# The last Fourier step of a spectral layer: each product in two halves of 64 columns, on two column tiles

## The chip, the cores and the metric

The kernel runs on one core of a Trainium2 chip. Its time is the device time of one execution in microseconds (us). The time before is a median of three runs; the profile is of one further execution. TensorE (PE) multiplies matrices: a weight load (LDWEIGHTS, shown as PEld) puts the stationary operand into the array, and a matmul then streams the moving operand through it into a PSUM bank. VectorE (DVE), ScalarE (ACT) and GpSimd (POOL) do the elementwise work, and SyncE (SP) starts the transfers (DMA).

## The reference

The input x has 8 batches of 3008 positions with 256 channels. Two layers follow each other: a mixing of the channels in the frequency domain, and a gated feed-forward network on each of the 24064 positions.

```python
X = np.fft.rfft(x, axis=1)
Yr = Xr @ w_r - Xi @ w_i + b_r
Yi = Xr @ w_i + Xi @ w_r + b_i
Yr = np.sign(Yr) * np.maximum(np.abs(Yr) - lam, 0.0)
Yi = np.sign(Yi) * np.maximum(np.abs(Yi) - lam, 0.0)
y = np.fft.irfft(Yr + 1j * Yi, n=3008, axis=1)
g = y @ w_gate
out = (g / (1 + np.exp(-g)) * (y @ w_val)) @ w_out
```

## The kernel before

The Fourier transforms are products with constant matrices. A length of 3008 is 47 times 64, so each transform has two steps. Forward: `stage_a` (line 395) transforms over 47 values with the weights `wa`; a transpose on DVE (line 400) turns the result; `second` (line 432) transforms over 64 values with `wf`. In the frequency domain two lines mix the channels (`total_product`, line 439, and `mix`, line 454), ACT gathers (line 466), and DVE and POOL clip and shrink (lines 499 and 500). Backward: `back` (lines 476 and 478) goes back over 64 values, the result is stored to a DRAM tensor `d2` in the order of frequencies k1, and `product` in `unit` (line 541) goes back over the 24 values of k1. This last one is the inverse over k1.

One unit of the inverse over k1 handles one batch b and one group u of four values of m (UM = 4, NU = 8 groups). It loads `z_in` from `d2`: 96 partitions (24 values of k1, real and imaginary parts, two halves) by 4 x 256 columns (four m, 256 channels). For each half cc of the channels, `product(cc)` then makes four matmuls, one for each m: the stationary operand is z_in with 128 channels as its columns, the moving operand are 94 columns of the constant `wo` for this m, and the result is 128 channels (partitions) by 94 positions, in a bank of its own (`ps_x0` or `ps_x1`), where the four matmuls lie beside each other. `copy(cc)` (line 552) copies the 376 columns of the bank to SBUF on ACT, and one transfer for both halves (line 565) writes them to `xt_d`, from where the feed-forward part reads its input. All operands of line 541 are f32, and in the program one f32 product of this kind is two weight loads and two matmuls. Batches 0 to 6 pass through `unit`: 7 x 8 units, 112 calls of `product`, 448 products. The last batch goes another way, in `inverse` (line 890) within the feed-forward part; there the same kind of product stays as it is.

The order of the first part is written out by a planner (`Plan`): each step has an engine, a cost, a due time and the steps that it needs. The steps of the inverse over k1 are "third0 n" and "third1 n" on PE, with a planned cost of 0.9, "xt0 n" and "xt1 n" on ACT, and "z_in n" and "out n" on SP. "third" needs the loaded z_in and the copy of the unit before out of the same bank; "xt" needs "third". The planner lays the steps out by these costs, and the kernel issues them in that order under a manual schedule. From the step "second 95" on (LOOSE = 95), the steps are issued outside the manual schedule. The feed-forward part (`gated_ffn`, products in line 655) begins where the transforms end; it reads what `xt_d` holds.

Of the kernel before, what the change touches and what calls it, by code (L numbers as in the profile page):

```python
# [17 lines left out]
P = 128  # L18
B = 8
SEQ = 3008  # L20
C = 256
# [225 lines left out]
def transform(ctx, tc, front, ring, last, ps_, feed, xp, w_r, w_i, cb, wup_raw, wdn_raw, ca, cf, ci, co, w21, wup_d, wdn_d, xt_d, d2):  # L247
    nc = tc.nc
# [276 lines left out]
    def unit(n):  # L525

        b, u = divmod(n, NU)
        key = (Z_FIRST + n * NP / NU if n < Z_LATE else Z_AT + (n - Z_LATE) * Z_STEP) * SLOT
        made = {}
        rows = d2.get(b)  # L530

        def load():
            t = made["z_in"] = last.tile([P, UM * C], F32, name="z_in", tag="z_in", bufs=3)
            rows = d2[b].rearrange("k (q m) c -> (k q) (m c)", m=NM)
            nc.sync.dma_start(t[:96], rows[:, u * UM * C : (u + 1) * UM * C])

        def product(cc):
            ps = made[cc] = ps_.tile([P, T], F32, name=f"ps_x{cc}")
            for i in range(UM):
                m = u * UM + i  # L540
                nc.tensor.matmul(  # L541
                    ps[:, i * 94 : (i + 1) * 94],
                    lhsT=made["z_in"][:96, i * C + cc * P : i * C + (cc + 1) * P],
                    rhs=box["wo"][:, m * 94 : (m + 1) * 94],
                    start=True,
                    stop=True,
                )

        def copy(cc):
            if "xt" not in made:  # L550
                made["xt"] = last.tile([P, 2, UT], F32, name="xt", tag="xt")
            nc.scalar.copy(made["xt"][:, cc, :], made[cc][:, :UT])

        old = lambda name, i: f"{name} {n - i}" if n >= i else None
        plan.add(f"z_in {n}", "SP", 0.5, key - 1.5 * SLOT, [f"store {b * NP + NP - 1}", old("third1", 3), "wo" if not n else None], load, 5.5)
        for cc in range(2):
            plan.add(f"third{cc} {n}", "PE", 0.9, key + (0.6 + 0.15 * cc) * SLOT, [f"z_in {n}", old(f"xt{cc}", 1)] + ([f"third0 {n}"] if cc else []), lambda cc=cc: product(cc))
            plan.add(f"xt{cc} {n}", "ACT", 0.36, key + (0.8 + 0.15 * cc) * SLOT, [f"third{cc} {n}", old("out", 2)] + ([f"xt0 {n}"] if cc else []), lambda cc=cc: copy(cc))
        plan.add(
            f"out {n}",  # L560
            "SP",
            0.45,
            key + 1.2 * SLOT,
            [f"xt1 {n}"],
            lambda: nc.sync.dma_start(xt_d[b][:, :, u * UT : (u + 1) * UT], made["xt"]),
            4.0,
        )

    box = {}
# [412 lines left out]
```

## Time and profile before

| What | Value |
|---|---|
| median of 3 runs | 2637.27 us (2637.2 to 2637.51) |
| the profiled execution: time | 2638.41 us |
| the profiled execution: span of its instructions | 2636.6 us |
| mean granted TensorE clock | 0.999 |
| line 541 in the stretch from 117 to 590 us: matmul records | 896, 115.25 us busy |
| line 541 in the same stretch: weight loads | 896, 111.44 us busy |
| line 655 (feed-forward), largest group of matmuls | 4032, 1038.1 us busy |
| line 890 (last batch), matmul records | 128, 18.1 us busy |

Times in the profile count from the start of the span. Matmul and weight-load records overlap each other, since the array is pipelined; the busy time of a group is the sum of the lengths of its records and may be longer than the time in which they pass. How far two starts lie apart tells what one of them really holds. A form such as "96*128 96x94" reads: 96 rows and 128 columns of the array in use, and 96 partitions by 94 elements streamed.

### The profile page before, as it was taken

What the parts mean: (1) busy time and instruction counts of PE and PEld (TensorE: products, weight loads), DVE (VectorE), ACT (ScalarE), POOL (GpSimd) and SP (SyncE); (2) the same over time, 40 slices, a digit from 0 to 9 for tenths busy, and PEclk for the clock granted to TensorE, in tenths of its full rate; (3) what the DMA queues carried; (4) which work ended last, traced back from release to release, by engine and by line L of the source; (5) the groups of instructions that cost most, each with busy time, mean ns of one, the idle gap of its engine ahead of it and who ended that gap; (6) DMA issues with size and microseconds to landing.
All of it is one profiled execution on the core that took longest, in us unless ns stands there. A gap on an engine that the chain in (4) does not pass through costs nothing.

```text
span 2636.6 us, 39325 instructions
## 1 busy us (share of the span) xinstructions
PE 2624.9 (100%) x13170; PEld 2206.3 (84%) x13170; DVE 2087.7 (79%) x3033; ACT 1713.4 (65%) x3344; POOL 2048.2 (78%) x1574
## 2 busy tenths in 40 slices
PE   9999999999999999999999999999999999999999
PEld 6888888898888888888888888888888888888899
DVE  6998788657787778777877878787878887888787
ACT  4777777786666666666666666656666666666665
POOL 3666665457888888888888888888888888888886
PEclk9999999999999999999999999999999999999999
DMA  6577766765544454445444444454444444444453
GB/s 191 180 257 231 235 226 224 242 196 195 182 165 151 149 165 158 153 145 165 164 149 149 164 166 154 145 165 165 146 145 161 160 152 150 151 159 159 150 176 127
DMA packets 141402, 452.54 MB, mean 172 GB/s; under 512 B 13776, under 2 KB 61616, under 8 KB 141104
## 3 DMA queue, kind: packets, MB, share of 16 engines
q1 hardware_dynamic: 141200, 450.02, 51.2%
q8 instruction: 105, 1.72, 0.3%
q14 instruction: 97, 0.79, 0.1%
HBM read 359.01 MB, written 90.96 MB: 171 GB/s over the span
## 4 chain that ended last, share of the span: by engine, by line
PE 98%; ACT 1%; DVE 0%; DMA 0%; POOL 0%; issue 0%; SPq 0%; ACTq 0%; DVEq 0%
PE bank L655 76%; PE mixb L454 5%; PE ps_a L395 4%; PE ps_x L541 4%; PE ps_b L432 3%; PE ps_s L439 3%; PE ps_z L478 2%; PE bank L890 1%; ACT hidden L800 0%; DMA x_first<-xp 0%; PE ps_z L476 0%; ACT t L466 0%; DVE f_lo L492 0%; DVE y_lo L502 0%; DVE wsum L299 0%
## 5 line engine op out<-in xcount | busy, mean ns | idle before, releaser
L655 PE MATMUL bank<-x_near,wup 128*128 128x512 f32 (+1 forms) x4032 | 1038.1, 386 | 0.6 <-DVE bank L829 0.3
L675 POOL TENSOR_TENSOR h_parts<-more,h_parts 128x512 fp32r<-128x512 f32 (+1 forms) x572 | 847.6, 1494 | 110.5 <-ACT h_parts L671 96.9
L655 PEld LDWEIGHTS bank<-x_near,wup 128*128 128x128 f32 x4032 | 750.5, 188 | 152.2 <-DVE bank L829 4.2
L655 PE MATMUL bank<-h_parts,wdn 128*128 128x512 f32 (+1 forms) x3021 | 835.7, 385 | 0.4 <-DVE h_parts L675 0.4
L675 POOL TENSOR_TENSOR h_parts<-hidden,h_parts 128x512 fp32r<-128x512 f32 (+1 forms) x431 | 564.9, 1322 | 206.4 <-ACT h_parts L671 187.0
L655 PEld LDWEIGHTS bank<-h_parts,wdn 128*128 128x128 f32 x3021 | 564.6, 188 | 109.3 <-DVE h_parts L675 0.7
L671 ACT CAST h_parts<-hidden 128x512 fp32r<-128x512 f32 (+1 forms) x433 | 266.0, 615 | 450.3 <-DVE hidden L802 450.3
L655 PE MATMUL bank<-x_parts,wup 128*128 128x512 f32 (+1 forms) x2016 | 526.6, 384 | 0.0
L802 DVE TENSOR_TENSOR hidden<-hidden,bank 128x512 f32<-128x512 f32 (+1 forms) x576 | 376.2, 675 | 77.8 <-PE bank L655 69.5
L655 PEld LDWEIGHTS bank<-x_parts,wup 128*128 128x128 f32 x2016 | 375.1, 188 | 71.5 <-DVE bank L829 1.8
L696 DVE TENSOR_TENSOR sums<-sums,bank 128x512 f32<-128x512 f32 (+1 forms) x357 | 240.4, 673 | 243.2 <-PE bank L655 243.2
L671 ACT CAST h_parts<-more 128x512 fp32r<-128x512 f32 (+1 forms) x572 | 349.6, 611 | 39.4 <-DVE more L666 28.1
L800 ACT ACTIVATE hidden<-bank 128x512 f32<-128x512 f32 (+1 forms) x432 | 252.7, 585 | 114.2 <-PE bank L655 113.9
L666 DVE TENSOR_TENSOR more<-hidden 128x512 f32<-128x512 f32 (+1 forms) x286 | 292.1, 1060 | 0.0
L666 DVE TENSOR_TENSOR more<-hidden,more 128x512 f32<-128x512 f32 (+1 forms) x286 | 258.3, 903 | 0.0
L500 POOL TENSOR_TENSOR t<-t,y 128x512 f32<-128x512 f32 x96 | 129.8, 1352 | 139.5 <-DVE y L499 132.9
L807 ACT COPY bank<-bank 128x512 f32<-128x512 f32 (+1 forms) x288 | 161.6, 561 | 109.2 <-DVE hidden L802 103.8
L829 DVE TENSOR_TENSOR bank<-hidden,bank 128x512 f32<-128x512 f32 (+1 forms) x288 | 197.0, 684 | 37.9 <-PE bank L655 26.0
L466 ACT COPY t<-mixb 64x256 f32<-64x256 f32 x384 | 141.2, 368 | 58.8 <-PE mixb L454 53.9
L815 ACT COPY hidden<-bank 128x512 f32<-128x512 f32 (+1 forms) x288 | 167.6, 582 | 2.5
L494 POOL TENSOR_TENSOR f_lo<-f,f_hi 128x256 fp32r<-128x256 f32 x96 | 90.8, 946 | 79.9 <-ACT f_hi L493 78.0
L214 POOL TENSOR_TENSOR x_near<-xf,x_near 128x512 fp32r<-128x512 f32 (+1 forms) x112 | 143.1, 1293 | 5.6 <-PE bank L655 4.8
(102 smaller groups left out, 3339.6 us busy)
## 6 DMA issues: line engine op xcount, KB each, us to landing
wup<-wup_d SPq DMA_DIRECT2D x288, 896.0 KB, 4.6
out<-o SPq DMA_DIRECT2D x88, 256.0 KB, 6.0
scratch<-xp SPq DMA_DIRECT2D x116, 192.0 KB, 3.2
d<-z SPq DMA_DIRECT2D x84, 256.0 KB, 2.6
z_in<-d SPq DMA_DIRECT2D x56, 384.0 KB, 3.7
xt_d<-xt SPq DMA_DIRECT2D x56, 376.0 KB, 3.9
xf<-xt_d SPq DMA_DIRECT2D x15, 1024.0 KB, 6.7
wup_d<-wup SPq DMA_DIRECT2D x12, 896.0 KB, 4.4
```

The lines of the kernel that those rows point to most:

```text
L214: low = lambda: eng.tensor_tensor(part[:, 1, :h], src, f32(part[:, 0, :h]), op=ALU.subtract)
L466: nc.scalar.copy(t()[64 * half : 64 * half + 64, k * C : (k + 1) * C], mixb[64 * k : 64 * k + 64, half * C : (half + 1) * C])
L655: nc.tensor.matmul(o, lhsT=weights[w], rhs=parts[x], start=start and i == 0, stop=stop and i == 2, skip_group_check=True)
L666: v.tensor_tensor(at(o, h), at(a, h), at(b, h), op=ALU.subtract)
L671: act.copy(pair[i][:, 0, :h], at(i, h))
L675: eng.tensor_tensor(pair[i][:, 1, :h], at(i, h), f32(pair[i][:, 0, :h]), op=ALU.subtract)
L696: v.tensor_tensor(o, o, spare[:, :h], op=ALU.add)
L800: act.activation(at(i, h), src, AF.Silu)
L802: v.tensor_tensor(at(i, h), at(i, h), src, op=ALU.mult)
L807: act.copy(b3[:, :h], b1[:, :h])
L815: act.copy(m5, b2[:, :h])
L829: v.tensor_tensor(b2[:, :h], m5, b3[:, :h], op=ALU.add)
```

## The change

Each product of line 541 is made as two, of 64 columns of z each. The first writes partitions 0 to 63 of the bank, the second partitions 64 to 127; the start of the output's partitions sets the column tile of the array on which a matmul runs. Both stream the same 94 columns of `wo`. The operands, the result, the copy out of the bank and the planned costs stay as they are. The order is: both records of the first half, then both of the second, then the next m.

```diff
             for i in range(UM):
                 m = u * UM + i
-                nc.tensor.matmul(
-                    ps[:, i * 94 : (i + 1) * 94],
-                    lhsT=made["z_in"][:96, i * C + cc * P : i * C + (cc + 1) * P],
-                    rhs=box["wo"][:, m * 94 : (m + 1) * 94],
-                    start=True,
-                    stop=True,
-                )
+                for side in range(2):
+                    col = i * C + cc * P + 64 * side
+                    nc.tensor.matmul(
+                        ps[64 * side : 64 * side + 64, i * 94 : (i + 1) * 94],
+                        lhsT=made["z_in"][:96, col : col + 64],
+                        rhs=box["wo"][:, m * 94 : (m + 1) * 94],
+                        start=True,
+                        stop=True,
+                    )
```

## The prediction

> **What bounds the kernel now.** I read the page first, for the share of each engine and for the chain of work that ended last.
>
> ```profile
> span 2636.6 us, 39325 instructions
> PE 2624.9 (100%) x13170; PEld 2206.3 (84%) x13170; DVE 2087.7 (79%) x3033; ACT 1713.4 (65%) x3344; POOL 2048.2 (78%) x1574
> PE 98%; ACT 1%; DVE 0%; DMA 0%; POOL 0%; issue 0%; SPq 0%; ACTq 0%; DVEq 0%
> PE bank L655 76%; PE mixb L454 5%; PE ps_a L395 4%; PE ps_x L541 4%; PE ps_b L432 3%; PE ps_s L439 3%; PE ps_z L478 2%; PE bank L890 1%; ACT hidden L800 0%; DMA x_first<-xp 0%; PE ps_z L476 0%; ACT t L466 0%; DVE f_lo L492 0%; DVE y_lo L502 0%; DVE wsum L299 0%
> ```
>
> TensorE carries 98% of the chain, and line 541, the only line that the change touches, has 4% of it: about 105 us. The first question is then where line 541 runs, and whether anything but TensorE holds that stretch. The view of one line gives its first and last start, the view of windows the busy time there, and the view of the tile ps_x the copies that read its results.
>
> ```profile
> L541 PEld LDWEIGHTS ps_x<-wo,z_in x896: 187/192/192, 117.6 to 588.6; 96*128 96x128 f32 x180
> L541 PE MATMUL ps_x<-wo,z_in x896: 244/275/275, 117.8 to 588.7; 96*128 96x94 f32 x180
> ```
>
> ```profile
> 117.00:590.00 473.00, 472.89 (x3361) 420.42 (x3360) 364.79 (x608) 362.16 (x842) 279.27 (x261) 1.00 0.70 228
> ```
>
> ```profile
> L552 ACT COPY xt<-ps_x x112: 464/473/507, 119.0 to 590.2; 128x376 f32<-128x376 f32 x112
> ```
>
> The columns of the window row are length, then PE, PEld, DVE, ACT and POOL busy, granted clock, DMA share and GB/s. From 117 to 590 us TensorE is busy for 472.89 of 473.00 us at a granted clock of 1.00; DVE (364.79) and ACT (362.16) have over 100 us to spare. So time added on TensorE here is added to the end in full, and time saved there is saved up to what the other engines allow. The 112 copies of line 552 are 112 blocks of line 541 (seven batches, eight groups, two channel halves); each block makes 4 products, and 896 matmul records are 8 a block. One f32 product is therefore two pairs of a weight load and a matmul.
>
> Now the inside of a block. The timeline of the matmuls (start, length, group, count), then the weight loads of the same block:
>
> ```profile
> 200.65 0.28 PE L454 MATMUL mixb<-wm_lo,f_hi 128*128 128x256 f32 x1
> 200.77 1.03 PE L541 MATMUL ps_x<-wo,z_in 96*128 96x94 f32 x8
> 201.58 0.48 PE L478 MATMUL ps_z<-y_hi,wi_hi 128*128 128x512 f32 x1
> ...
> 202.35 1.03 PE L541 MATMUL ps_x<-wo,z_in 96*128 96x94 f32 x8
> 203.22 1.13 PE L432 MATMUL ps_b<-wf,d 128*128 128x128 f32 x8
> ```
>
> ```profile
> 200.65 0.98 PEld L541 LDWEIGHTS ps_x<-wo,z_in 96*128 96x128 f32 x8
> ```
>
> ```profile
> 200.77 0.36 PE L541 MATMUL ps_x<-wo,z_in 96*128 96x94 f32 x2
> ```
>
> A record is 0.275 us long but they overlap, so what counts is the distance of the starts. From the first matmul of a block to the first of the next line: 201.58 - 200.77 = 0.81 us, and 203.22 - 202.35 = 0.87 us in the other; 112 blocks of these are 91 to 97 us. The weight loads follow each other every (0.98 - 0.19) / 7 = 0.113 us. The last row is a shorter window onto the same block, showing its first two matmuls: the second starts 0.36 - 0.275 = 0.085 us after the first. Its weights were loaded ahead, behind the previous line's matmul. So streaming 94 f32 columns holds the array for 0.085 us, loading 128 f32 columns of weights takes 0.113 us, and **line 541 is bound by its weight loads**, not by its streams. Each pair wastes about 0.028 us of the stream.
>
> **The change part by part.** Each product becomes two, of 64 columns of z each, into partitions 0 to 63 and 64 to 127 of the same bank. Per block, 8 pairs become 16: 896 weight loads and 896 matmuls more over the kernel. The 94 columns of wo are streamed once for each half. DMAs, copies, waits and the order of the blocks written out by the plan stay as they are, and the data read and written are the same; the copy of line 552 still waits for the block's last matmul. No wait and no queue entry on another engine is added. Everything therefore hangs on three unknown prices on TensorE. Every matmul of this trace is 128 columns wide, so none of the three is shown.
>
> First, the **weight load of 64 columns**. Below stands half of the present one, 0.113 / 2 = 0.0565 us, above the same 0.113 us (if the price did not hang on the columns). The nearest row for the dependence is the same for 96 and 128 rows, with equal columns:
>
> ```profile
> L541 PEld LDWEIGHTS ps_x<-wo,z_in 96*128 96x128 f32 x896 | 111.4, 191 | 2.2
> L432 PEld LDWEIGHTS ps_b<-wf,d 128*128 128x128 f32 x768 | 102.7, 196 | 16.6 <-issue 9.7 <-ACT f_hi L493 2.2 <-DVE d L400 0.5
> ```
>
> Rows change the mean by 5 ns only (191 against 196), so the columns are what is left to carry it, and I take half. Two halves loaded in turn then cost what one whole costs now: 4 x 0.0565 = 0.226 us a product against 2 x 0.113 = 0.226 us, a change of 0. The Trainium skill, page "TensorE: Matmul & The Clock Gate", section "LDWEIGHTS (loading the stationary operand)", also has the time go by columns and not by rows; by its rate, 128 columns are 0.107 us (measured here: 0.113 us) and 64 would be an estimated 0.053 us. That is the Trainium skill's figure, and the sum by it is the same to 1 or 2 us.
>
> Second, the **streams**. If the two halves can be streamed side by side, in program order, a product's four matmuls (high and low part of half 0, then of half 1) take two stream times, since the low part of one half and the high part of the next fall together: 2 x 0.085 = 0.17 us, and the loads at 0.226 us still bind unless they too run side by side. If the halves take turns, it is 4 x 0.085 = 0.34 us. The ends are thus -0.056 us a product (448 x 0.056 = -25 us) and +0.114 us (448 x 0.114 = +51 us; counted by blocks, 15 x 0.085 + 0.06 = 1.335 against 0.81 us, 112 x 0.525 = +59 us, which I use). I take the middle case, streams that overlap and loads in turn: 0, since the streams (0.17 us) lie behind the loads (0.226 us); without that cover it is the second end. A gain beyond -25 us is excluded by the order of the matmuls.
>
> Third, the **passage from full width to half width and back**, at both ends of each block. Going from line 454 (128 rows) to line 541 (96 rows) costs nothing now: 200.77 - 200.65 = 0.12 us, which is the spacing inside line 454 as well. Leaving costs 0.06 us: the last matmul starts at 200.77 + 1.03 - 0.275 = 201.525, the next line at 201.58. So one end is 0. The other end is a wait until the array has emptied: the next matmul starts only when the record before it ends.
>
> ```profile
> L454 PE MATMUL mixb<-wm_lo,f_hi 128*128 128x256 f32 x384 | 108.4, 282 | 0.0
> L541 PE MATMUL ps_x<-wo,z_in 96*128 96x94 f32 x896 | 115.2, 271 | 0.0
> ```
>
> Entering: 0.282 - 0.12 = 0.16 us. Leaving: 0.275 - 0.06 = 0.215 us. Together 0.38 us a block, 112 x 0.38 = **+42 us**; were the next weight load to wait as well (some 0.1 us at either end), up to 112 x 0.6 = +67 us. The row change is the nearest passage in the trace and is free, but in it the 128 columns remain one array. Here the columns are divided, weights still waiting for full width and weights for half width would lie in the array together, and the ends of the overlapping records are as far as their work reaches. I take +42 us. The Trainium skill, page "TensorEngine Tiling (Array Packing)", section "Key Properties", states that changing the tiling mode, as against the tile, drains TensorE. No run here shows it yet. It speaks against this change.
>
> The sum: loads 0, streams 0, passages +42 us. The profiled execution took 2638.41 us (its span is 2636.6 us), 1.1 us over the median of 2637.27 us; the sum is 2638.4 + 42 = 2680.4 us there, and 2637.3 + 42 = 2679 us as a median. I say 2680 us. The last blocks, some 18 after 550 us, lie partly where the scheduler and not the written order places them, and could stand differently; at 0.4 us each that is worth a few us.
>
> **The rivals.** (1) **Side by side, and no price for the passage**: loads of the two halves run beside each other too, the product takes 0.17 us, 448 x -0.056 = -25 us, 2612 us. This one ends on the other side: faster. It decides wherever the passages cost less than 25 / 112 = 0.22 us a block. DVE and ACT leave room for it (364.79 and 362.16 us of 473). For it speaks the measured 0.028 us of each pair in which the stream waits for weights; against it, that no row shows two loads under way closer than 0.11 us. The Trainium skill, page "TensorE: Matmul & The Clock Gate", section "Part 3: Packing small matmuls — row/col tiling", has matmuls on different column tiles run at once; by the Trainium skill it would thus be this case or the forecast, and not the third. No run here shows it. (2) **Streams overlap, loads in turn, free passage**: 0, 2637 us. With side-by-side loads but the passage at +42 us: -25 + 42 = +17 us, 2654 us. (3) **The halves take turns**, so the change does not do what the two column tiles say: +59 us, 2696 us. For it speaks that in the whole of the quoted block no two matmuls start closer than 0.085 us. (4) Turns and passages: +59 + 42 = +101 us, 2738 us; the same +101 us comes if a load keeps its 0.113 us whatever its width (8 x 0.113 = 0.90 us a block more).
>
> **How the numbers follow.** The forecast (2680 us, its own range 2650 to 2705 us by the passage at 0.1 to 0.6 us) has 0.32. Rival 1 (2612) has 0.23; a free passage with loads in turn (2637) 0.11; loads beside each other with the passage paid (2654) 0.09; turns (2696) 0.16; turns and passages, or loads of unchanged price (2738), 0.09. What can be told from no change is about 0.2%, 5 us. Faster: rival 1 and a little of the mixed cases, 0.24. Same: the free passage, 0.12. Slower: the rest, 0.64. The range goes from 2610 us to 2720 us, so that it leaves out the last case alone.
>
> **What would show it.** In the changed kernel line 541 should have 1792 weight loads and 1792 matmuls of 64 columns. In the timeline of one block: a forecast that holds shows starts about 0.056 us apart on average inside the block, and 0.28 us or so between the last matmul before the block and its first, likewise behind it. Rival 1 shows an inside of 0.65 us for 16 matmuls and 0.06 to 0.12 us at the ends; turns show 0.085 us throughout. TensorE must stay at its 473 of 473 us with a longer stage, and the stage after 590 us must keep its length of 2046 us. The prediction is wrong if the ends of the blocks show no gap, or if the stage's length does not follow from the blocks, above all if the sequencer cannot deliver twice as many instructions and gaps of "issue" appear in front of them; the present trace cannot say, since 0.113 us a pair is its densest stretch.

## The result, and the profile after

The change makes the kernel slower: 2651.21 us (median of 4 runs, 2650.91 to 2652.39) against 2637.39 us, a ratio of 1.0053 with a 95% interval of 1.0036 to 1.0070, or +13.8 us. The profiled execution took 2650.91 us, with a span of 2649.1 us, 12.5 us more than before. The sign was forecast, the size was not: +42 us stood in the prediction.

The page of the changed kernel; line 543 is now what line 541 was, and line 657 what line 655 was.

```profile
span 2649.1 us, 41116 instructions
PE 2637.6 (100%) x14066; PEld 2186.9 (83%) x14066; DVE 2085.2 (79%) x3033; ACT 1712.5 (65%) x3344; POOL 2046.4 (77%) x1574
PE 98%; ACT 1%; DVE 0%; DMA 0%; issue 0%; SPq 0%; ACTq 0%; DVEq 0%
PE bank L657 76%; PE mixb L454 5%; PE ps_a L395 4%; PE ps_b L432 4%; PE ps_x L543 3%; PE ps_s L439 3%; PE ps_z L478 3%; PE bank L892 1%; ACT hidden L802 0%; DMA x_first<-xp 0%; PE ps_z L476 0%; DVE f_lo L492 0%; ACT t L466 0%; DVE d L400 0%; DVE bank L853 0%
```

TensorE bounds the kernel as before, and 896 matmuls and as many loads were added. What stands out is that line 543 has *less* of the chain (3%) than line 541 had (4%), although the kernel is slower. The view of windows (length, then busy time of PE, PEld, DVE, ACT and POOL) shows where the time lies: the stage with line 543 now ends at about 602 us, 12 us later, TensorE is busy in it all the time, and what follows is as long as it was.

```profile
117.00:602.00 485.00, 484.60 (x4251) 399.70 (x4249) 363.65 (x607) 362.88 (x840) 277.81 (x261) 1.00 0.69 222
602.00:2646.00 2044.00, 2041.75 (x9208) 1703.13 (x9204) 1628.78 (x2277) 1277.88 (x2336) 1711.99 (x1257) 1.00 0.47 158
```

One block in the timeline of the matmuls (start, length, group, count), to be set beside the block shown in the prediction:

```profile
258.25 0.28 PE L454 MATMUL mixb<-wm_lo,f_hi 128*128 128x256 f32 x1
258.45 0.87 PE L543 MATMUL ps_x<-wo,z_in 96*64 96x94 f32 x16
259.26 0.86 PE L432 MATMUL ps_b<-wf,d 128*128 128x128 f32 x5
```

Inside, 16 matmuls take 0.87 us where 8 whole ones took 1.03 us: the block itself is shorter. At its ends it loses. From the last matmul before the block to its first are 258.45 - 258.25 = 0.20 us (0.12 us before the change). From the block's last start, 258.45 + 0.87 - 0.244 = 259.08, to the next line are 0.18 us. Before the change that depended on the line behind: 0.06 us with line 478, as in the block of the prediction, and 0.11 us with line 432. So a block with lines 454 and 478 around it is the one to compare:

```profile
333.91 0.28 PE L454 MATMUL mixb<-wm_lo,f_hi 128*128 128x256 f32 x1
334.12 0.87 PE L543 MATMUL ps_x<-wo,z_in 96*64 96x94 f32 x16
334.92 0.50 PE L478 MATMUL ps_z<-y_hi,wi_hi 128*128 128x512 f32 x1
```

The whole visit, from the last start before it to the first start behind it, takes 334.92 - 333.91 = 1.01 us against 201.58 - 200.65 = 0.93 us: 112 x 0.08 = +9 us. The next start behind is late as well: where line 432 follows it comes 0.22 us after the first in place of 0.15 us, elsewhere 0.02 us later than before. Counted up to this second start, and over all whole blocks of the two traces, a visit has grown from 1.19 to 1.29 us: 112 x 0.10 = +11 us.

Shorter windows onto the block at 258.45 us, two of the matmuls and two of the weight loads, show how it becomes shorter:

```profile
258.45 0.30 PE L543 MATMUL ps_x<-wo,z_in 96*64 96x94 f32 x2
...
258.45 0.38 PE L543 MATMUL ps_x<-wo,z_in 96*64 96x94 f32 x4
```

```profile
258.45 0.14 PEld L543 LDWEIGHTS ps_x<-wo,z_in 96*64 96x64 f32 x2
...
258.45 0.20 PEld L543 LDWEIGHTS ps_x<-wo,z_in 96*64 96x64 f32 x4
```

Two matmuls, the longest of them 0.295 us, end 0.30 us after the first start: in the nanoseconds of the trace they start 7 ns apart. So do their two loads, which are 0.133 us long and over in 0.14 us. **Streams and loads of the two column tiles run side by side.** Four loads are over in 0.20 us, the last of them 0.136 us long, so that the second pair of loads starts 0.06 us behind the first: a load of 64 columns holds its tile for about half of the 0.113 us of a whole one. The next pair of matmuls follows 0.13 us after the first, all further pairs about every 0.080 us, so that a product, two pairs, takes 0.16 us where it took 0.223 us.

A count over the whole trace: the distance from each matmul's start to the next one's, summed by the lines at which it begins and ends (us; "the line" is line 541 or its successor).

| Kernel | within the line | into it | out of it | other transform lines | feed-forward |
|---|---|---|---|---|---|
| before | 83.9 | 16.5 | 8.1 | 476.8 | 2045.2 |
| after | 70.6 | 28.5 | 20.3 | 479.5 | 2044.0 |
| after less before | -13.3 | +11.9 | +12.2 | +2.7 | -1.1 |

The last row adds up to 12.5 us before rounding, the whole growth of the span. Most of the +2.7 us is the passage once more, the late second start behind a block: 24 x 0.07 = 1.7 us where line 432 follows. After 570 us, where the order is not the written one, other lines break into some blocks: the traces have 114 visits before the change and 118 after it.

### The profile page after: what moved, and what is told of

Same layout as the page of the kernel before. It is cut to its first block, busy times and chain, and to the rows that moved or that the text cites. A ratio compares the mean times of both kernels' runs of the same rounds, so it can differ in the third digit from the quotient of the medians.

```text
span 2649.1 us, 41116 instructions
## 1 busy us (share of the span) xinstructions
PE 2637.6 (100%) x14066; PEld 2186.9 (83%) x14066; DVE 2085.2 (79%) x3033; ACT 1712.5 (65%) x3344; POOL 2046.4 (77%) x1574
## 4 chain that ended last, share of the span: by engine, by line
PE 98%; ACT 1%; DVE 0%; DMA 0%; issue 0%; SPq 0%; ACTq 0%; DVEq 0%
PE bank L657 76%; PE mixb L454 5%; PE ps_a L395 4%; PE ps_b L432 4%; PE ps_x L543 3%; PE ps_s L439 3%; PE ps_z L478 3%; PE bank L892 1%; ACT hidden L802 0%; DMA x_first<-xp 0%; PE ps_z L476 0%; DVE f_lo L492 0%; ACT t L466 0%; DVE d L400 0%; DVE bank L853 0%
```

## The experiments

Eight kernels were run, each beside the kernel before; their ratios are to that.

| Run | median us | ratio, 95% interval |
|---|---|---|
| after | 2651.2 | 1.0053, 1.0036 to 1.0070 |
| both channel halves in one step, halves of z | 2632.5 | 0.9983, 0.9974 to 0.9992 |
| both channel halves in one step, whole products | 2637.2 | 1.0000, 0.9991 to 1.0008 |
| both in one step, first channel half alone in halves of z | 2642.7 | 1.0019, 1.0010 to 1.0028 |
| every other product in halves | 2698.0 | 1.0228, 1.0214 to 1.0242 |
| quarters | 2648.2 | 1.0042, 1.0029 to 1.0055 |
| both in one step, quarters | 2631.4 | 0.9976, 0.9967 to 0.9985 |
| loops exchanged | 2693.2 | 1.0212, 1.0198 to 1.0225 |
| two products a side | 2656.7 | 1.0071, 1.0059 to 1.0084 |

**Fewer passages, the same work.** Theory A is that each passage to and from half width costs, and the block itself gains; theory B that the doubled number of instructions costs. A unit's two channel halves are made in one step, so that 32 half-width matmuls stand together and there are 56 visits in place of 112.

```diff
-        for cc in range(2):
-            plan.add(f"third{cc} {n}", "PE", 0.9, key + (0.6 + 0.15 * cc) * SLOT, [f"z_in {n}", old(f"xt{cc}", 1)] + ([f"third0 {n}"] if cc else []), lambda cc=cc: product(cc))
-            plan.add(f"xt{cc} {n}", "ACT", 0.36, key + (0.8 + 0.15 * cc) * SLOT, [f"third{cc} {n}", old("out", 2)] + ([f"xt0 {n}"] if cc else []), lambda cc=cc: copy(cc))
+        plan.add(f"third1 {n}", "PE", 1.8, key + 0.6 * SLOT, [f"z_in {n}", old("xt1", 1)], lambda: [product(cc) for cc in range(2)])
+        for cc in range(2):
+            plan.add(f"xt{cc} {n}", "ACT", 0.36, key + (0.8 + 0.15 * cc) * SLOT, [f"third1 {n}", old("out", 2)] + ([f"xt0 {n}"] if cc else []), lambda cc=cc: copy(cc))
```

> The changed kernel with both channel halves of a unit made in one step, so that 56 blocks of 32 half-width matmuls stand in place of 112 blocks of 16; instructions and operands are the same. Theory A (the passage between full and half width costs 0.09 us at the entry and 0.11 us at the exit, the rest of a block is gained): 56 blocks fewer x 0.20 us = 11 us less, and some 3 us more from the slow second start of each block; 2637 to 2640 us. Theory B (the loss hangs on the doubled number of instructions, not on the passages): the number is unchanged, 2651 us.

It took 2632.5 us, 18.8 us less than the changed kernel and 4.9 us less than the kernel before. Theory B is out: the number of instructions is the same. Theory A has the direction, but its 2637 to 2640 us are too high: it counts the bare entry and exit, 0.20 us, and a visit costs more, as the lines below give it. The control is the same edit on the kernel before:

> The kernel before with the same merging of the two channel halves into one step, products left whole: a control for the merging alone. Entering and leaving a block costs nothing there, so both theories expect 2637 us within 3 us. If it moves by more, the merging changes the order of the other steps and the run with halves has to be read against this one.

It took 2637.2 us: the merging alone moves nothing that the runs can tell. One visit of each, first with halves, then whole:

```profile
270.85 0.28 PE L454 MATMUL mixb<-wm_lo,f_hi 128*128 128x256 f32 x1
271.06 1.52 PE L543 MATMUL ps_x<-wo,z_in 96*64 96x94 f32 x32
272.51 0.50 PE L478 MATMUL ps_z<-y_hi,wi_hi 128*128 128x512 f32 x1
```

```profile
255.07 0.28 PE L454 MATMUL mixb<-wm_lo,f_hi 128*128 128x256 f32 x1
255.19 1.92 PE L541 MATMUL ps_x<-wo,z_in 96*128 96x94 f32 x16
256.89 0.48 PE L478 MATMUL ps_z<-y_hi,wi_hi 128*128 128x512 f32 x1
```

From the last start before to the first start behind: 272.51 - 270.85 = 1.66 us with halves, 256.89 - 255.07 = 1.82 us whole. With the two visits of 4 products between the same lines (1.01 and 0.93 us) that makes four points, and two straight lines go through them. A whole product costs (1.82 - 0.93) / 4 = 0.223 us, and the visit itself 0.93 - 4 x 0.223 = 0.04 us. A product in halves costs (1.66 - 1.01) / 4 = 0.163 us, and the visit itself 1.01 - 4 x 0.163 = **0.36 us**. Half width costs 0.32 us a visit and gives back 0.06 us a product; it pays from 0.32 / 0.06 products on, between 5 and 6. The change puts 4 into a visit. The 56 visits fewer are 56 x 0.32 = 18 us, close to the 18.8 us measured.

**The same price, foretold.** Two lines through two points each fit always, so the price was put to a new case: both channel halves in one step, but the first alone in halves of z.

```diff
-                for side in range(2):
+                for side in range(2 - cc):
                     col = i * C + cc * P + 64 * side
+                    wide = 64 + 64 * cc
                     nc.tensor.matmul(
-                        ps[64 * side : 64 * side + 64, i * 94 : (i + 1) * 94],
-                        lhsT=made["z_in"][:96, col : col + 64],
+                        ps[64 * side : 64 * side + wide, i * 94 : (i + 1) * 94],
+                        lhsT=made["z_in"][:96, col : col + wide],
```

> Both channel halves of a unit in one step; the four products of the first channel half in halves of 64 columns, the four of the second whole, so that a block of 8 products has one entry and one exit of half width and 4 half-width products. Theory A (a visit to half width costs 0.32 us whatever is done in it, and each half-width product gives 0.06 us back, as worked out from blocks of 4 and of 8 products): 0.32 - 4 x 0.06 = 0.08 us a block over the whole products, 56 x 0.08 = +4.5 us on 2637.2 us, 2641.7 us. Theory B (each product in halves brings its own share of the gain that 8 of them brought): half way between 2637.2 and 2632.5 us, 2635 us.

Measured: 2642.7 us. All 8 in halves make the kernel faster, 4 of 8 make it slower than none: what costs is the visit, not the product. Its visit in the timeline takes 258.00 - 256.08 = 1.92 us, where the two lines give 0.36 + 4 x 0.163 + 4 x 0.223 = 1.90 us.

```profile
256.08 0.28 PE L454 MATMUL mixb<-wm_lo,f_hi 128*128 128x256 f32 x1
256.29 1.93 PE L544 MATMUL ps_x<-wo,z_in 96*64 96x94 f32 x24
258.00 0.48 PE L478 MATMUL ps_z<-y_hi,wi_hi 128*128 128x512 f32 x1
```

**More passages, fewer instructions.** The first and third product of a block in halves, the others whole, otherwise as the changed kernel.

```diff
-                for side in range(2):
+                for side in range(2 - i % 2):
+                    wide = 64 + 64 * (i % 2)
                     col = i * C + cc * P + 64 * side
...
-                        ps[64 * side : 64 * side + 64, i * 94 : (i + 1) * 94],
-                        lhsT=made["z_in"][:96, col : col + 64],
+                        ps[64 * side : 64 * side + wide, i * 94 : (i + 1) * 94],
+                        lhsT=made["z_in"][:96, col : col + wide],
```

> The changed kernel with the first and third product of a block in halves, the second and fourth whole: 12 pairs of weight load and matmul a block in place of 16, but two entries and two exits of half width in place of one and one. Theory A (passages cost 0.09 us and 0.11 us): one entry and one exit more a block, 112 x 0.20 = +23 us; two whole products instead of halves lose 2 x 0.06 us, 112 x 0.12 = +14 us; 2688 us, within 8 us. Theory B (the loss hangs on the number of instructions): a quarter fewer, half of the 14 us is given back, 2644 us.

It took 2698.0 us, 46.8 us over the changed kernel, beyond the 2688 us of theory A and its 8 us, and far from the 2644 us of theory B. The expectation counted 0.20 us for one visit more, the bare entry and exit. With the 0.32 us of the lines above, 112 x 0.32 = 36 us and 112 x 2 x 0.06 = 13 us for two products not in halves give 2700 us. Three windows onto one block:

```profile
270.50 0.38 PE L544 MATMUL ps_x<-wo,z_in 96*64 96x94 f32 x4
...
270.50 0.66 PE L544 MATMUL ps_x<-wo,z_in 96*64 96x94 f32 x5
...
270.50 0.77 PE L544 MATMUL ps_x<-wo,z_in 96*64 96x94 f32 x6
```

The four half-width records of the first product have ended 0.38 us after its start, that is at 270.88. The fifth record, the first whole one (a record of 0.348 us), ends 0.66 us after it and so starts 0.31 us after it, about 0.17 us behind the last half-width start; the sixth (0.275 us) starts at 0.77 - 0.275 = 0.495 us, another 0.18 us later, where whole products that follow each other have 0.11 us. A passage thus delays two starts, not one: the first waits, and the second is late behind it. In the trace the first load of the new width starts only with its first matmul (1 ns before it, median of 14 such blocks), where inside a run of whole products it starts 0.08 us ahead.

**More tiles.** Four quarters of 32 columns, on four column tiles.

```diff
-                for side in range(2):
-                    col = i * C + cc * P + 64 * side
+                for side in range(4):
+                    col = i * C + cc * P + 32 * side
...
-                        ps[64 * side : 64 * side + 64, i * 94 : (i + 1) * 94],
-                        lhsT=made["z_in"][:96, col : col + 64],
+                        ps[32 * side : 32 * side + 32, i * 94 : (i + 1) * 94],
+                        lhsT=made["z_in"][:96, col : col + 32],
```

> The changed kernel with each product in four quarters of 32 columns on four column tiles: 32 weight loads and 32 matmuls a block in place of 16 and 16. Theory A (inside a block the stream of 94 f32 columns is the limit, 0.080 us, whatever number of tiles runs beside each other; the passages are unchanged): 2651 us within 4 us. Theory B (each instruction costs): again 14 us more, 2665 us or over.

It took 2648.2 us. The block of 32 loads and 32 matmuls is as long as that of 16 (0.86 and 0.87 us), and four matmuls start within some 20 ns:

```profile
257.82 0.29 PE L543 MATMUL ps_x<-wo,z_in 96*32 96x94 f32 x4
...
257.82 0.86 PE L543 MATMUL ps_x<-wo,z_in 96*32 96x94 f32 x32
```

Neither the number of instructions nor the width of a load sets the pace inside, which stays at about 0.080 us a group. It is what the streams should take, as theory A has it, by a longer stream of f32 in the kernel before:

```profile
204.19 1.02 PE L395 MATMUL ps_a<-scratch,wa 96*128 96x512 f32 x2
```

The second of these matmuls (a record of 0.59 us) starts 1.02 - 0.59 = 0.43 us after the first, and 0.43 x 94 / 512 = 0.08 us. That is an estimate, and one rival stays: inside the line a matmul starts 0.08 us after its own load in all three widths (128, 64 and 32 columns), and no run changed the number of streamed columns, so a fixed lead of the load over its matmul could set the same pace.

Of the 3 us that quarters are faster than halves, half is found in the blocks. The second group starts 0.085 us behind the last start of the first in place of 0.125 us, but the four starts of a group are spread over 20 ns in place of 7, so that the block is shorter by 0.013 us only: 112 x 0.013 = 1.5 us. Most of the rest may be the visits that are broken up after 570 us, 115 in place of 118 in all. Quarters and the merged step together:

> Both edits that helped together: the two channel halves of a unit in one step, and four quarters of 32 columns in place of two halves of 64. Theory A (stream and passages are the limits): the run with both channel halves in one step, 2632.5 us, less 56 x 0.04 us for the earlier second start of a block that the run with quarters showed: 2630 us. Theory B (64 loads and 64 matmuls within one block are more than the sequencer can hold ahead): slower than 2632.5 us.

This was the fastest kernel, 2631.4 us, 0.24% below the kernel before (0.15% to 0.33%). Its lead over the merged step with halves, 1.1 us, is smaller than the runs can tell: their intervals overlap. It is not slower, as theory B had it.

**How far apart the two tiles may be in the program.** First with the loops exchanged, all four products of the first 64 columns and then all four of the second:

```diff
-            for i in range(UM):
-                m = u * UM + i
-                for side in range(2):
+            for side in range(2):
+                for i in range(UM):
+                    m = u * UM + i
```

> The changed kernel with the loops exchanged: in each block all four products of the first 64 columns, then all four of the second 64. The two column tiles are then 4 products apart in the program. Theory A1 (matmuls of the two tiles overlap only if they are neighbours in the program): a block takes 16 starts of 0.080 us in turn in place of 8 pairs, 15 x 0.080 + 0.17 = 1.37 us against 0.80 us, 112 x 0.57 = +64 us, 2715 us. Theory A2 (each tile works off what is queued for it): the overlap stays, 2651 us.

It took 2693.2 us, 42 us over the changed kernel: neither 2715 nor 2651. Windows onto one block, up to 0.38 and 0.69 us after its start, and whole:

```profile
268.78 0.62 PE L543 MATMUL ps_x<-wo,z_in 96*64 96x94 f32 x5
...
268.78 0.92 PE L543 MATMUL ps_x<-wo,z_in 96*64 96x94 f32 x12
268.78 1.25 PE L543 MATMUL ps_x<-wo,z_in 96*64 96x94 f32 x16
```

In the first 0.38 us 5 matmuls start, in the next 0.31 us 7, and the last 4 alone again: the second tile begins beside the fifth matmul of the first, three matmuls ahead of its turn in the program, and has its own remainder to itself at the end. The trace names no tile; the sixth start, 6 ns behind the fifth, is taken for the second tile's, since one tile's own starts lie about 0.080 us apart. So the overlap reaches a few matmuls ahead, not further. With two products a side, the two tiles are four matmuls apart:

```diff
-            for i in range(UM):
+            for i, side in ((0, 0), (1, 0), (0, 1), (1, 1), (2, 0), (3, 0), (2, 1), (3, 1)):
                 m = u * UM + i
-                for side in range(2):
```

> The changed kernel with the halves in the order first half of products 0 and 1, second half of products 0 and 1, and so on: the two column tiles are four matmuls apart in the program, where they are two apart in the changed kernel and eight apart in the run with the loops exchanged, whose second tile began beside the fifth matmul of the first. Theory A1 (only neighbours overlap): part of the overlap is lost, 2665 us or over. Theory A2 (a tile starts up to about four matmuls ahead of its turn): the overlap stays whole, 2651 us within 4 us.

It took 2656.7 us, 5.5 us over the changed kernel. That is outside the 4 us of theory A2 and well under the 2665 us of A1: most of the overlap stays, and the block grows a little. Of the three orders tried, two apart, as the change has it, is the best.

## Why the prediction was wrong

- **TensorE bounds the stage, and added time goes to the end in full**: right. 484.60 of 485.00 us busy, the stage 12 us longer, the rest unchanged.
- **Weight loads of 64 columns cost half, and the two halves load in turn: 0**: this step failed, in its second part. Half was right (0.06 us). But the loads run side by side (two starts 7 ns apart), so that they no longer bind. The quoted loads of the kernel before follow each other every 0.113 us, but all of them fill the whole array; that two smaller ones would still take turns did not follow from it.
- **Streams that overlap, hidden behind the loads: 0**: the overlap was right; with the loads no longer above them a pair of matmuls takes 0.080 us, near the 0.085 us that the prediction gave the stream. It read that figure with the second matmul's weights loaded ahead; they were not: only the first load of that block comes early (0.12 us before the first matmul), the second starts with the first matmul. Together these two terms were put at 0 and are 448 x -0.06 = -27 us, about the lower end of -25 us that the prediction named for them.
- **Passages, 0.38 us a block, +42 us**: right in kind and nearly in size. The lines through the visits give 0.32 us, 112 x 0.32 = +36 us. It falls otherwise than foretold: the entry costs 0.09 us and not 0.16, the exit 0.11 us and not 0.215 (0.06 us before line 432). Of the 0.12 us that are left, the second start of a half-width block takes 0.05 us (0.13 us behind the first in place of 0.08), and the early second start of a whole block, which is lost, 0.03 us (0.083 us in place of 0.112); the remainder is not split up. The wait ends before the modelled end of the records: the first start comes 0.21 us after that of a record of 0.28 us. The rule of the Trainium skill, page "TensorEngine Tiling (Array Packing)", section "Key Properties", is that a change of the mode drains TensorE, and a change of the tile alone does not. The trace agrees so far: each change of the width brings a wait, and the two tiles of a block start 7 ns apart. Whether the array is empty by then, no run shows. The price of there and back is 0.32 us by the runs.
- **The sum**: -27 + 36 = +9 us by blocks, +11 us with the late second start behind them, +12.5 us in the profile. It is the case that stood among the rivals as side-by-side loads with the passage paid, 2654 us, with a chance of 0.09. The forecast had the cost and left out the gain. Its own range began at 2650 us, for a passage of 0.1 us; that 2651 us lies in it is luck, since the passage cost three times as much and the gain made up for it.
- **The signs that were named**: the block showed the inside of rival 1 (0.87 - 0.24 = 0.63 us, named as 0.65), and ends of 0.21 and 0.17 us, between those of rival 1 and the 0.28 us of the forecast.
- **Halves that take turns**: out; the changed kernel's pairs and the run with the loops exchanged, where they do take turns for a part and lose 42 us, show it.
- **The sequencer as a limit**: out as far as tried, 64 loads and 64 matmuls in one visit.

## What to carry to other kernels

In this kernel a narrower column tile takes weight loads off the path, because the tiles load and stream side by side, but every visit to it has a price at its two ends. Count the products per visit, not the products: 4 lose, 8 gain, and the break-even worked out from them lies between 5 and 6. When an edit that should gain loses, look at the length of the group itself: here it had become shorter, and the loss stood in the starts before and behind it.

## What was not expected of the hardware

Loads of two column tiles overlap although both use the same 96 rows (starts 7 ns apart). The time until a matmul of another width may start follows the stream before it: with line 454 (256 columns) ahead the first start is 0.21 us behind, with line 478 (512 columns) ahead 0.33 us (means over 29 visits each), in place of 0.12 and 0.23 us. A matmul of the second tile can start before matmuls of the first tile that stand earlier in the program, before three of them in the run with the loops exchanged. Why the first pair of a visit is followed after 0.125 us with halves, but after 0.085 us with quarters, was not tried further.
